# f32 routing tables, first expert's transposes inside its first half, and v cast behind its loads, in a fused attention and expert kernel

## The chip, the cores and the metric

The kernel runs on one core of a Trainium2 chip. The metric is the time of one execution on the device, in microseconds. The core has five engines that run their own instruction queues side by side: TensorE (PE, with its weight loads PEld), VectorE (DVE), ScalarE (ACT), GpSimd (POOL) and SyncE (SP). POOL, SP and ACT also issue DMA transfers.

## The reference

Block-causal attention over 8 batches, 8 heads, 576 positions and 64 channels, followed by a hard mixture of experts:

```python
scores = (1 / sqrt(64)) * q @ k.T                       # per batch and head
scores = where(pos[:, None] // 64 >= pos[None, :] // 64, scores, -1e9)
attn = exp(scores - max); attn = attn / sum(attn)
x = (attn @ v).transpose(0, 2, 1, 3).reshape(4608, 512) # 8 heads x 64 side by side
for e in range(8):                                      # each row has one expert
    rows = domain_id == e
    out[rows] = relu(x[rows] @ w1[e]) @ w2[e]           # 512 -> 1024 -> 512
```

The inputs and the output are f32; the kernel computes its matrix products on f16 operands.

## The kernel before, in words

The program is written in a fixed order: every engine executes its own instructions in the order in which the Python code emits them, and only semaphores hold it back.

**Attention** (lines 455 to 529) runs over 32 pairs of heads, four pairs to a batch, in 33 steps. In a step, PE computes the scores of pair p in three groups (`emit_G`, L348 and L374), ACT takes the exponential of each (`emit_exp`, L353), PE transposes q and k of pair p+2 (`emit_T`, L336), DVE copies those transposes out of PSUM (L340), and PE multiplies the weights of pair p-1 with v (`emit_pv`, L399 and L404, called by `emit_P` and `emit_Q`). DVE then divides by the row sums, which come from columns of ones in v (`emit_norm`, L427 and L428), and the rows x are stored to a DRAM buffer `x_rows` by SP (`store_x`, `store_w`).

v comes as f32 into one of three staging tiles `vst`, batch b into `vst[b % 3]`. Batch 0 is loaded by SP, all others by POOL, in nine transfers each (`load_v`, L79 and L83); POOL also issues the loads of q and k (`load_qk`, L70). `cast_v` (L115) makes f16 tiles `vS` of it in three instructions, on ACT for batch 0 and on POOL for the others. For the diagonal blocks of 64, `emit_VE` (L437) copies parts of v into a second tile `VE` with two DVE instructions a batch, which at present read `vS`. `loads(p)` at the end of step p sets the order on POOL: at step max(0, 4b-10) the q and k of batch b, five of its v transfers, the cast of batch b-1, and the remaining four transfers. At step 20 come the cast of the last batch and the weights of the first expert, one piece in each step up to 27.

**Routing.** In the first steps DVE counts for each row its place among the rows of its expert (`routing`). From step 2 on, `inverse` builds the table of row numbers per expert slot in slices between the steps: one-hot matrices `Hq`, `Hh` and `L` by comparisons and products on DVE (L204, L207, L211, L217), multiplied by PE (L229) and summed by DVE (L233, L235), then closed with L247 to L255. The operands `iota_h`, `lo_h` and `ub` and the matrices are f16.

**The last pair** (step 32) has its normalisation split by PSUM bank: `emit_norm(prev, 0, 1)` after `emit_P`, with a store, and `emit_norm(st, 1, 2)` after the last matmuls in `emit_Q`, with two stores. Then 36 dummy matmuls (`warm`, L533) keep PE running until the first rows are gathered.

**Experts.** For each of eight experts POOL gathers five blocks of 128 rows (L547), PE transposes them (`transpose_block`, L557) and ACT copies the result into `xT` (L560). `mm1` multiplies with w1 for eight column groups fc, with ACT applying ReLU into `hT` (L579, L585), and `mm2` with w2, block by block, while the next expert's blocks are transposed (L596); DVE copies the result out (L602) and POOL scatters it (L603). The first expert is done in two halves of 320 rows: blocks 0 to 2 are transposed and `mm1` runs on the first half, then blocks 3 and 4 and the second half. A loop at the end serves experts with more than 640 rows; its code is there, and on these inputs it does not run.

Of the kernel before, what the change touches and what calls it, by code (L numbers as in the profile page):

```python
# [9 lines left out]
F32 = mybir.dt.float32  # L10
F16 = mybir.dt.float16
# [7 lines left out]
def kernel(  # L19
# [82 lines left out]
    up = const.tile([128, 128], F16, name="up")  # L102
    make_upper_triangular(nc, up[:], 1.0, diag=False)
    load_qk(0, 1, HP)
    p_f = const.tile([128, 1], F32, name="p_f")
    nc.gpsimd.iota(out=p_f[:], pattern=[[0, 1]], base=4, channel_multiplier=NJ,
                   allow_small_or_imprecise_dtypes=True)
# [5 lines left out]
    def cast_v(fn, b):  # L113
        for pr, cs in ((128, slice(0, 2)), (128, slice(2, 4)), (64, slice(4, 5))):
            fn(  # L115
                out=vS[b % 3][0:pr, cs, :, 2:130],
                in_=vst[b % 3][0:pr, cs].rearrange(
                    "p c (g i) d -> p c g (i d)", i=2))
# [37 lines left out]


    ones_sq = const.tile([128, 128], F16, name="ones_sq")
    lo_h = const.tile([128, NJ], F16, name="lo_h")
    u_f = const.tile([128, NJ], F32, name="u_f")  # L160
    base_f = const.tile([128, 1], F32, name="base_f")
    n_i = const.tile([1, 1], I32, name="n_i")
# [25 lines left out]


    def inverse(sb, pp, tag, ncols, base, tok):  # L190
        ub = sb.tile([128, NJ], F16, name="ub", tag="ub")
        nc.vector.tensor_scalar(
            out=ub[:], in0=u_f[:], scalar1=base, scalar2=None, op0=ALU.subtract)
        inv = sb.tile([128, 2, ncols], F32, name="inv", tag="inv")
        fi = inv[:].rearrange("p a c -> p (a c)")
        sh = [128, NQ, ncols]
        ts = {}

        def hot(qt):
            js = slice(NQ * qt, NQ * qt + NQ)  # L200
            Hq = sb.tile([128, NQ, ncols], F16, name="Hq", tag="Hq", bufs=2)
            Hh = sb.tile([128, NQ, 2, ncols], F16, name="Hh", tag="Hh", bufs=2)
            L = sb.tile([128, NQ, 128], F16, name="L", tag="L", bufs=2)
            nc.vector.tensor_tensor(  # L204
                out=Hq[:], in0=iota_h[:, 0:ncols].unsqueeze(1).to_broadcast(sh),
                in1=ub[:, js].unsqueeze(2).to_broadcast(sh), op=ALU.is_equal)
            nc.vector.tensor_scalar(  # L207
                out=Hh[:, :, 0], in0=Hq[:], scalar1=p_f[:, 0:1], scalar2=None,
                op0=ALU.mult)
            yield  # L210
            nc.vector.tensor_tensor(  # L211
                out=Hh[:, :, 1], in0=Hq[:],
                in1=iota_h[:, js].unsqueeze(2).to_broadcast(sh), op=ALU.mult)
            yield
            for j in range(0, NQ, 3):
                sl = [128, 3, 128]
                nc.vector.tensor_tensor(  # L217
                    out=L[:, j : j + 3], in0=iota_h[:].unsqueeze(1).to_broadcast(sl),
                    in1=lo_h[:, js][:, j : j + 3].unsqueeze(2).to_broadcast(sl),
                    op=ALU.is_equal)  # L220
                yield
            ts[qt] = (L, Hh)

        def add(qt):
            L, Hh = ts[qt]
            ps = pp.tile([128, 512], F32, name=tag, tag=tag, bufs=2)
            pv = ps[:, 0 : 2 * ncols]
            for j in range(NQ):
                nc.tensor.matmul(  # L229
                    out=pv, lhsT=L[:, j], rhs=Hh[:, j].rearrange("p a c -> p (a c)"),  # L230
                    start=(j == 0), stop=(j == NQ - 1))
            if qt == 0:
                nc.vector.tensor_copy(out=fi, in_=pv)  # L233
            else:
                nc.vector.tensor_tensor(out=fi, in0=fi, in1=pv, op=ALU.add)  # L235

        for qt in range(4):
            first = True
            for _ in hot(qt):
                yield  # L240
                if first and qt:
                    add(qt - 1)
                first = False
        yield
        add(3)
        yield
        nc.vector.tensor_tensor(  # L247
            out=inv[:, 0], in0=inv[:, 0], in1=inv[:, 1], op=ALU.add)
        nc.vector.tensor_scalar(
            out=inv[:, 1], in0=inv[:, 0], scalar1=0.0, scalar2=1.0e6,  # L250
            op0=ALU.is_equal, op1=ALU.mult)
        nc.vector.scalar_tensor_tensor(
            out=tok[:, 0], in0=inv[:, 0], scalar=-4.0, in1=inv[:, 1],
            op0=ALU.add, op1=ALU.add)
        nc.vector.tensor_scalar(  # L255
            out=tok[:, 1], in0=tok[:, 0], scalar1=float(N - 1), scalar2=None,
            op0=ALU.min)
        yield
# [20 lines left out]
    def routing():  # L279
# [9 lines left out]
        for i, w in enumerate((ones_sq, up)):  # L289
# [24 lines left out]
        lo_i = asb.tile([128, NJ], I32, name="lo_i")  # L314
        nc.vector.tensor_scalar(out=lo_i[:], in0=ri[:], scalar1=127, scalar2=None,
                                op0=ALU.bitwise_and)
        nc.vector.tensor_copy(out=lo_h[:], in_=lo_i[:])
        nc.vector.tensor_scalar(out=cnt[:], in0=inc[:, :, NJ - 1], scalar1=-1.0,
                                scalar2=None, op0=ALU.add)
        nc.vector.memset(base_f[:], 0.0)  # L320
# [93 lines left out]
    def emit_Q(st):  # L414
        emit_pv(st, 3, 4)
        emit_pv(st, 4, 0)
        if st["p"] < npair - 1:
            emit_norm(st, 0, 2)
        else:
            emit_norm(st, 1, 2)  # L420

    def emit_norm(st, b0, b1):
        hp = st["p"] % HP
# [10 lines left out]
    def emit_VE(b):  # L434
        for i in range(2):
            cs = slice(2 + 64 * i, 66 + 64 * i)
            nc.vector.tensor_copy(  # L437
                out=VE[b % 2][64 * i : 64 * i + 64, :, :, cs],
                in_=vS[b % 3][0:64, :, :, cs])


    def store_w(b, w0, w1, c0, c1, eng):
# [20 lines left out]

    def loads(p):
        fn = nc.gpsimd.tensor_copy
        for b in range(2, B):
            if p == max(0, 4 * b - 10):
                load_qk(b)
                load_v(nc.gpsimd, b, range(0, 5))
                cast_v(fn, b - 1)  # L470
                load_v(nc.gpsimd, b, range(5, H + 1))
        if p == 4 * B - 12:
            cast_v(fn, B - 1)
            for e in range(4):
                wts.append(load_expert(e))
        if 4 * B - 12 <= p < 4 * B - 4:
            wts[0][p - 4 * B + 12]()
# [3 lines left out]
    for p in range(npair + 1):  # L481
# [13 lines left out]
            emit_G(1, st)  # L495
        if prev is not None:
            emit_P(prev)
            if prev["p"] == npair - 1:
                emit_norm(prev, 0, 1)
                store_w(B - 1, 0, 3, DM - 128, DM, nc.sync)  # L500
        if p < npair:
            emit_G(2, st)
        if prev is not None:
# [66 lines left out]
    def new_hT():  # L570
        return msb.tile([128, 8, CAP], F16, name="hT", tag="hT", bufs=2)

    def mm1(xT, hT, w1h, halves=(0, 1)):
        hw = CAP // 2
        for fc in range(8):
            ph = mps.tile([128, 2, 512], F32, name="ph", tag="ph", bufs=2)
            for dc in range(4):
                for i in halves:
# [56 lines left out]
    for e in range(E):  # L635
# [4 lines left out]
                f()  # L640
        hT = new_hT()
        if e == 0:
            for i, blks in enumerate(((0, 1, 2), (3, 4))):
                for blk in blks:
                    transpose_block(xgs[0], xT, blk)
                    if blk < 2:
                        warm(mps.tile([128, 512], F32, name="po", tag="po", bufs=2), 5)
                mm1(xT, hT, w1s[0], (i,))
        else:
            mm1(xT, hT, w1s[e])  # L650
        nxt = None
# [59 lines left out]
```

## Time and profile before

| | us |
|---|---|
| median of 4 runs | 322.93 |
| lowest, highest | 320.32, 325.6 |
| the profiled execution's own time | 318.33 |
| its span, first to last instruction | 316.6 |

| engine | busy us | share of the span | instructions |
|---|---|---|---|
| PE | 272.7 | 86% | 3668 |
| PEld | 177.1 | 56% | 3668 |
| DVE | 145.2 | 46% | 260 |
| ACT | 168.6 | 53% | 248 |
| POOL | 206.1 | 65% | 274 |

The shares are means over two stages: attention with the table until about 141 us, and the experts from about 150 us. The page also cuts the span into 40 slices; the view by stretches, used below, gives for a stretch the busy time of each engine with its number of instructions, the clock that was granted to PE, the mean busy share of the DMA engines and GB/s. In the view in order of time a row has its start, its duration, the engine, the line, the operation with its operands, how many instructions are joined in it, and in brackets the idle time of the engine just before it and what ended that. Matmuls are pipelined, so that a PE that is busy need not be at its peak.

### The profile page before, as it was taken

To read this page: it belongs to the slowest core of one execution; us is meant where nothing else is said; L and a number is where in the kernel's file an instruction comes from. 1 tells how busy PE (TensorE), PEld (TensorE's weight loads), DVE (VectorE), ACT (ScalarE), POOL (GpSimd) and SP (SyncE) were. 2 spreads that over 40 slices of the span, in tenths; PEclk is the share of its full clock that TensorE was granted. 3 is DMA by queue.
4 is the path that set the end of the run, shared out by engine and by line. 5 is a ranking of instruction groups with operands and counts; after the bars stand their busy time and mean duration, and the time that the engine had idled before them with its cause. 6 is when DMAs were issued, how large, how long until landed. Compare 5 with 4: busy or idle time off the path is not lost. (4 is left out here: it accounts for less than half of the span.)

```text
span 316.6 us, 8633 instructions
## 1 busy us (share of the span) xinstructions
PE 272.7 (86%) x3668; PEld 177.1 (56%) x3668; DVE 145.2 (46%) x260; ACT 168.6 (53%) x248; POOL 206.1 (65%) x274
## 2 busy tenths in 40 slices
PE   2598787959798999869989999999999999999920
PEld 1366565637575767644555656656565665756510
DVE  2878889999987888740003222030302203030210
ACT  5658575738777989840573444526344452635200
POOL 8659989899795800005888557878688686762230
PEclk9999798788989999998999999999999999999995
DMA  7999999997998593221788999898979989651120
GB/s 159 201 222 200 186 269 189 262 203 151 251 185 242 126 209 92 79 70 53 146 192 192 210 249 230 172 231 199 250 180 180 266 180 213 191 192 58 49 106 0
DMA packets 36488, 55.68 MB, mean 176 GB/s; under 512 B 9854, under 2 KB 22654, under 8 KB 36448
## 3 DMA queue, kind: packets, MB, share of 16 engines
q0 software_dynamic: 26128, 49.17, 72.5%
q1 hardware_dynamic: 10176, 5.90, 6.7%
q8 instruction: 30, 0.49, 0.6%
q14 instruction: 10, 0.08, 0.1%
q10 hardware_dynamic: 144, 0.03, 0.1%
HBM read 67.15 MB, written 15.20 MB: 260 GB/s over the span
## 5 line engine op out<-in xcount | busy, mean ns | idle before, releaser
L353 ACT ACTIVATE A<-ps 128x1024 f16<-128x1024 f32 (+1 forms) x96 | 83.1, 884 | 37.2 <-PE ps L348 25.7
L602 DVE COPY osb<-po 128x512 f32<-128x512 f32 x40 | 27.7, 692 | 132.6 <-PE po L596 104.3
L547 POOL DMA_INDIRECT xg<-x_rows,tok x40 | 40.6, 1015 | 47.6 <-issue 47.3
L585 ACT ACTIVATE hT<-ph 128x640 f16<-128x640 f32 (+1 forms) x72 | 46.4, 644 | 38.3 <-PE ph L579 37.4
L603 POOL DMA_INDIRECT out_dram<-osb,tok x40 | 40.7, 1017 | 34.7 <-DVE osb L602 17.6
L596 PE MATMUL po<-w2h,hT 128*128 128x512 f16 x240 | 56.7, 379 | 0.0
L579 PE MATMUL ph<-xT,w1h 128*128 128x320 f16 x384 | 54.2, 299 | 1.7 <-ACT xT L560 1.7
L79 POOL DMA_DIRECT2D vst<-in_v_dram x56 | 42.8, 791 | 11.4 <-DMA kh<-in_k_dram 5.8
L560 ACT COPY xT<-pt 128x512 f16<-128x512 f16 x40 | 23.3, 585 | 50.0 <-PE pt L557 37.2
L579 PEld LDWEIGHTS <-w1h 128*128 128x128 f16 x384 | 37.5, 98 | 18.1 <-issue 3.1
L340 DVE COPY QK<-PT 128x576 f16<-128x576 f16 x64 | 45.4, 749 | 3.3 <-PE PT L336 3.0
L596 PEld LDWEIGHTS <-hT 128*128 128x128 f16 x320 | 29.9, 98 | 29.3
L348 PE MATMUL ps<-QK 64*128 64x512 f16 (+3 forms) x256 | 36.8, 326 | 2.8 <-ACT A L353 1.1
L404 PE MATMUL po<-vS,A 128*128 128x65 f16 x640 | 36.5, 200 | 1.1 <-issue 1.1
L399 PE MATMUL po<-VE,ATE 128*128 128x130 f16 x160 | 32.7, 231 | 4.1 <-DVE x L428 4.0
L404 PEld LDWEIGHTS <-A 128*128 128x128 f16 x640 | 31.9, 102 | 4.6 <-issue 4.5
L428 DVE TENSOR_TENSOR x<-po,rc 128x768 f16<-128x768 f32 (+1 forms) x33 | 30.8, 933 | 1.1
L336 PE MATMUL PT<-identh,kh 64*64 64x64 f16 x576 | 17.2, 205 | 8.9 <-DVE inv L235 4.3
L336 PE MATMUL PT<-identh,qh 64*64 64x64 f16 x576 | 17.0, 205 | 5.1 <-DVE QK L340 3.7
L399 PEld LDWEIGHTS <-ATE 128*128 128x128 f16 x160 | 15.9, 99 | 9.5 <-issue 7.4
L336 PEld LDWEIGHTS <-kh 64*64 64x64 f16 x576 | 15.2, 120 | 10.3 <-issue 8.3
L336 PEld LDWEIGHTS <-qh 64*64 64x64 f16 x576 | 13.7, 118 | 12.8 <-issue 10.9
(89 smaller groups left out, 284.3 us busy)
## 6 DMA issues: line engine op xcount, KB each, us to landing
vst<-in_v_dram POOLq DMA_DIRECT2D x63, 128.0 KB, 7.0
w1h<-in_moe_w_dram POOLq DMA_DIRECT2D x24, 256.0 KB, 6.2
w2h<-in_moe_w_dram POOLq DMA_DIRECT2D x24, 256.0 KB, 8.4
vst<-in_moe_w_dram POOLq DMA_DIRECT2D x16, 256.0 KB, 8.7
qh<-in_q_dram POOLq DMA_DIRECT2D x14, 288.0 KB, 5.9
kh<-in_k_dram POOLq DMA_DIRECT2D x14, 288.0 KB, 8.3
x_rows<-x SPq DMA_DIRECT2D x7, 512.0 KB, 8.1
vst<-in_v_dram SPq DMA_DIRECT2D x4, 256.0 KB, 5.7
```

Of the source, the lines that this page charges most:

```text
L79: eng.dma_start(out=vst[b % 3][:, 0:4, n], in_=v[b, n, 0:512, :].rearrange("(c p) d -> p c d", p=128))
L336: nc.tensor.transpose(out=PT[h, j], in_=src[h, hp, 64 * j : 64 * j + 64], identity=identh[h, h])
L340: nc.vector.tensor_copy(out=QK[:, s].rearrange("p (n j) -> p n j", j=9), in_=PT[:].rearrange("p j n -> p n j"))
L348: nc.tensor.matmul(out=o[:, i], lhsT=QK[h, 1, 128 * c : 128 * c + 128], rhs=QK[h, 0, 64 + 128 * c : S], start=True, stop=True)
L353: nc.scalar.activation(out=o, in_=i, func=AF.Exp, scale=0.125)
L399: nc.tensor.matmul(out=o[:, 1:131], lhsT=st["AE"][:, 128 * m : 128 * m + 128], rhs=VE[b % 2][:, m, hp, 1:131], start=True, stop=(m == 0))
L404: nc.tensor.matmul(out=o[:, 1 + 65 * i : 66 + 65 * i], lhsT=at_block(st, i, c, m), rhs=vS[b % 3][:, c, hp, 1 + 65 * i : 66 + 65 * i], star ...
L547: nc.gpsimd.indirect_dma_start(out=g[:, blk, :], out_offset=None, in_=xd, in_offset=bass.IndirectOffsetOnAxis(ap=tok[:, 1, blk : blk + 1], ...
L579: nc.tensor.matmul(out=ph[:, i, 0:hw], lhsT=w1_cols(w1h, dc, fc), rhs=xT[:, dc, hw * i : hw * i + hw], start=(dc == 0), stop=(dc == 3))
L585: nc.scalar.activation(out=hT[:, fc].rearrange("p (i n) -> p i n", i=2)[:, i0:i1], in_=ph[:, i0:i1, 0:hw], func=AF.Relu)
L596: nc.tensor.matmul(out=po[:], lhsT=hT[:, fc, 128 * blk : 128 * blk + 128], rhs=w2h[:, fc, :], start=(fc == 0), stop=(fc == 7))
L603: nc.gpsimd.indirect_dma_start(out=dst[blk], out_offset=bass.IndirectOffsetOnAxis(ap=tok[:, 0, blk : blk + 1], axis=0), in_=osb[:], in_off ...
```

## The change

Five things are edited. The tables `Hq`, `ub` and `lo` and the iota that they are compared with become f32 (a second iota on POOL); `Hh` and `L`, which PE reads, stay f16. `emit_VE` reads the f32 staging tile in batches 0 to 5, and `vS` only in the last two. `loads` issues all nine v transfers of a batch together and casts batch b at step max(1, 4b-4). The first normalisation of the last pair and its store move behind the last matmuls, into `emit_Q`. And the transposes of the first expert's blocks 3 and 4 are issued inside the first half's `mm1`, ahead of column groups 4 and 6.

```diff
+    iota_f = const.tile([128, 128], F32, name="iota_f")
+    nc.gpsimd.iota(out=iota_f[:], pattern=[[1, 128]], base=0, channel_multiplier=0,
+                   allow_small_or_imprecise_dtypes=True)
...
-    lo_h = const.tile([128, NJ], F16, name="lo_h")
+    lo_f = const.tile([128, NJ], F32, name="lo_f")
...
-        ub = sb.tile([128, NJ], F16, name="ub", tag="ub")
+        ub = sb.tile([128, NJ], F32, name="ub", tag="ub")
...
-            Hq = sb.tile([128, NQ, ncols], F16, name="Hq", tag="Hq", bufs=2)
+            Hq = sb.tile([128, NQ, ncols], F32, name="Hq", tag="Hq", bufs=2)
...
-                out=Hq[:], in0=iota_h[:, 0:ncols].unsqueeze(1).to_broadcast(sh),
+                out=Hq[:], in0=iota_f[:, 0:ncols].unsqueeze(1).to_broadcast(sh),
...
-                in1=iota_h[:, js].unsqueeze(2).to_broadcast(sh), op=ALU.mult)
+                in1=iota_f[:, js].unsqueeze(2).to_broadcast(sh), op=ALU.mult)
...
-                    out=L[:, j : j + 3], in0=iota_h[:].unsqueeze(1).to_broadcast(sl),
-                    in1=lo_h[:, js][:, j : j + 3].unsqueeze(2).to_broadcast(sl),
+                    out=L[:, j : j + 3], in0=iota_f[:].unsqueeze(1).to_broadcast(sl),
+                    in1=lo_f[:, js][:, j : j + 3].unsqueeze(2).to_broadcast(sl),
...
         if st["p"] < npair - 1:
             emit_norm(st, 0, 2)
-        else:
-            emit_norm(st, 1, 2)
+            return
+        emit_norm(st, 0, 1)
+        store_w(B - 1, 0, 3, DM - 128, DM, nc.sync)
+        emit_norm(st, 1, 2)
...
                 out=VE[b % 2][64 * i : 64 * i + 64, :, :, cs],
-                in_=vS[b % 3][0:64, :, :, cs])
+                in_=vst[b % 3][0:64].rearrange(
+                    "p c (g i) d -> p c g i d", i=2)[:, :, :, i]
+                if b < B - 2 else vS[b % 3][0:64, :, :, cs])
...
-        for b in range(2, B):
-            if p == max(0, 4 * b - 10):
+        for b in range(1, B):
+            if b > 1 and p == max(0, 4 * b - 10):
                 load_qk(b)
-                load_v(nc.gpsimd, b, range(0, 5))
-                cast_v(fn, b - 1)
-                load_v(nc.gpsimd, b, range(5, H + 1))
+                load_v(nc.gpsimd, b, range(H + 1))
+            if p == max(1, 4 * b - 4):
+                cast_v(fn, b)
         if p == 4 * B - 12:
-            cast_v(fn, B - 1)
             for e in range(4):
...
-            if prev["p"] == npair - 1:
-                emit_norm(prev, 0, 1)
-                store_w(B - 1, 0, 3, DM - 128, DM, nc.sync)
...
-    def mm1(xT, hT, w1h, halves=(0, 1)):
+    def mm1(xT, hT, w1h, halves=(0, 1), between={}):
         hw = CAP // 2
         for fc in range(8):
+            if fc in between:
+                between[fc]()
...
-            for i, blks in enumerate(((0, 1, 2), (3, 4))):
-                for blk in blks:
-                    transpose_block(xgs[0], xT, blk)
-                    if blk < 2:
-                        warm(mps.tile([128, 512], F32, name="po", tag="po", bufs=2), 5)
-                mm1(xT, hT, w1s[0], (i,))
+            for blk in range(3):
+                transpose_block(xgs[0], xT, blk)
+                if blk < 2:
+                    warm(mps.tile([128, 512], F32, name="po", tag="po", bufs=2), 5)
+            mm1(xT, hT, w1s[0], (0,), {
+                4: lambda: transpose_block(xgs[0], xT, 3),
+                6: lambda: transpose_block(xgs[0], xT, 4)})
+            mm1(xT, hT, w1s[0], (1,))
```

The instructions on POOL, as built, change only so: in every batch the three casts stand behind all nine v transfers rather than behind five, and the last batch's casts stand behind the four w1 pieces of the first expert.

## The prediction

> **What bounds the kernel now.** I read the page first. Its chain of what ended last is no help, since it holds only the final 1.1 us, so I took the table by stretches and then the instructions in order of time.
>
> ```profile
> 40.00:60.00 20.00, 16.54 (x375) 12.16 (x369) 19.01 (x32) 13.00 (x18) 18.55 (x26) 0.83 1.08 247
> 60.00:80.00 20.00, 15.99 (x387) 11.86 (x385) 19.17 (x32) 13.30 (x20) 18.50 (x26) 0.91 0.96 184
> 120.00:140.00 20.00, 16.63 (x393) 12.21 (x392) 14.06 (x25) 16.62 (x24) 0.00 (x0) 1.00 0.15 49
> 200.00:240.00 40.00, 40.00 (x273) 24.74 (x272) 6.92 (x10) 19.07 (x30) 31.02 (x39) 1.00 0.94 206
> ```
>
> After the span the columns are PE, PEld, DVE, ACT, POOL. From 40 to 80 us DVE is busy for 38.2 of 40 us: while the routing table is built beside attention, DVE sets the pace. At 120 to 140, with the table and the loads done, a pair takes 3.0 us (the reciprocals of L427 at 131.51, 134.50, 137.50), with ACT busiest; a pair with an L437 copy still costs about 0.5 us in each of two steps (112.31 to 115.78 to 119.32 us between multiplications). So DVE time added before 105 us lengthens attention nearly one for one. From 180 to 280 us PE is full, and what starts the first expert earlier ends the kernel earlier.
>
> Part of DVE's time is not work. Its rows, then POOL's:
>
> ```profile
> 41.29 0.52 DVE L211 TENSOR_TENSOR Hh<-Hq,iota_h 128x360 f16<-128x360 f16 x1
> 53.45 3.63 DVE L211 TENSOR_TENSOR Hh<-Hq,iota_h 128x360 f16<-128x360 f16 x1
> 66.66 2.56 DVE L437 COPY VE<-vS 64x1280 f16<-64x1280 f16 x2
> 80.69 2.03 DVE L247 TENSOR_TENSOR inv<-inv 128x40 f32<-128x40 f32 x1
> 126.18 0.97 DVE L437 COPY VE<-vS 64x1280 f16<-64x1280 f16 x2
> 31.82 1.09 DVE L437 COPY VE<-vS 64x1280 f16<-64x1280 f16 x2 [0.84 <-POOL vS L115]
> ```
>
> ```profile
> 54.02 2.67 POOL L115 CAST vS<-vst 128x1024 f16<-128x1024 f32 x3
> 67.51 3.47 POOL L115 CAST vS<-vst 128x1024 f16<-128x1024 f32 x3
> 80.00 2.66 POOL L115 CAST vS<-vst 128x1024 f16<-128x1024 f32 x3
> 33.53 0.75 POOL L79 DMA_DIRECT2D vst<-in_v_dram  x1 [0.17 <-issue]
> ```
>
> The same L211 takes 0.52 us, or 3.63 when POOL's three casts run beside it, and it ends just after they do; L437 and L247 stretch in the same way. Operations that read PSUM (L340, L427, L428) do not. I count the loss as 3.1 at 53 us; 1.6 for L437 at 66 and, just behind it, 0.6 for L211 and 0.4 for L217; 2.1 at 81 to 83 (L247 and L249 against some 0.2 and 0.3); 0.5 for L437 at 86, beside a load. That is **8.3 us**, and 0.84 us more where the L437 copy waits for the cast outright.
>
> **The change, part by part.**
>
> *VE copied from the f32 staging tile (batches 0 to 5).* Twelve L437 copies, median 488 ns each with f16 input. Instructions of 360 (L204, 526 ns) and 384 elements (L217, 549 ns) give about 1 ns an element over some 150 ns fixed; so the f16 copy moves 1280 elements in 338 ns, four an element time. No DVE copy from f32 in SBUF is in the trace. It is bounded by 0.49 us (nothing changes) and by one element per ns, 1280 + 150 = 1.43 us. I take the value nearest to the same copy: equal bytes per ns, 2 x 338 + 150 = 0.83 us, 0.34 more. 12 x 0.34 = **+4.0 us** (0 to +11.3). All lie before 102 us and count in full. The wait on the cast goes: **-0.84 us**. Next behind it would be the load of v for batch 1, issued by 22.3 and, at 7 us to landing, there by about 29, before 31 us.
>
> *f32 tables.* The L204, L211 and L217 instructions (20 in all) already run at one element per ns; L309, 288 elements with an f32 input, takes 457 ns, the same rate. So nothing for them. L207, four times 399 ns for 360 elements, is faster than that rate; at L211's 524 ns it costs 4 x 0.125 = **+0.5 us** (0 to +0.5). The one iota more on POOL (0.33 us, like L98) stands at 7.7 us before loads that wait for transfers anyway (0.94 us at 11.22): nothing.
> The Trainium skill, "VectorE: DVE Perf Modes", section "The perf-mode tier table", speaks against this edit: two-input operations run at twice the f32 rate on 16-bit data. By it each L217 would take half its element time, and f32 would cost 20 x some 0.2 = 4 us. The row says 549 ns for 384 elements with 16-bit data, so there is nothing to lose; the operand that is broadcast is the likely reason. I go by the row.
>
> *Casts after all nine loads of v.* The order on POOL changes only so: a batch's three casts (2.66 us) move behind four more loads, and the last batch's behind four w1 pieces. As built, a load waits for the landing of the load eight issues before. Now the cast fills that wait (only 0.17 us idle at 33.53); afterwards it does not. The last load ends at 34.96, and the first cast starts there rather than at 29.12, so the q and k loads behind it slip by 2.7 us, in every batch. They are used far later (batch 3 is loaded at 35 and transposed from about 60 us): nothing. vS of batch 1 is ready at 37.6, its last part that PE reads at 37.0; PE reads it between 36.5 and 37.1: 0 (0 to +1.0).
> What moves is where casts meet DVE. I walk both engines forward with the durations above, a POOL round of about 14 us: casts at about 35, 49, 63.5, 80 and 95 us. They then meet an L217 (0.5 us), the batch 2 copy (2.3) and a table block (1.2), and nothing afterwards: 4.1 us instead of 8.3. But two of these five land within half a microsecond of an edge, so I take half of the gain: **-2.1 us** (-8.3 if no cast meets anything; +7.2 if five casts each cost the 3.1 seen at 53 us).
> A second rule, the box on DVE and SWDGE in "SBUF — State Buffer", section "SBUF: two separate sides", says that an f32 copy within SBUF keeps POOL from writing the descriptors of its loads. At 47.87, beside L437, two loads still take 1.28 us as elsewhere. By the rule POOL would lose up to 12 x 0.34 = 4 us, all of it before its idle 35 us at 110; no end moves.
>
> *First expert's transposes.*
>
> ```profile
> 158.82 0.61 PE L557 MATMUL pt<-identh,xg 128*128 128x128 f16 x8
> 159.35 1.07 ACT L560 COPY xT<-pt 128x512 f16<-128x512 f16 x2
> 160.48 4.94 PE L579 MATMUL ph<-xT,w1h 128*128 128x320 f16 x32 [1.04 <-ACT xT L560]
> ```
>
> Set inside the first half, the eight transposes cost PE the same, and the copies (0.58 us) lie between ReLUs that leave ACT 0.12 us free in each 0.62 us; a copy holds one ReLU back, and the second ph buffer covers that. Blocks 3 and 4 were requested at 149.55 and 150.85; with 4.4 us to land they are there by 155.3, before the new places at about 156.5 and 158. The 1.04 us wait goes: **-1.0 us** (0 to -1.2). The second half is then bound by PE.
>
> *Last pair's normalisation.*
>
> ```profile
> 140.36 0.22 PE L399 MATMUL po<-VE,ATE 128*128 128x130 f16 x1 [0.88 <-DVE x L428]
> 140.91 0.20 DVE L427 RECIPROCAL rc<-po 128x6 f32<-128x6 f32 x1 [0.61 <-PE po L399]
> 145.50 1.10 POOL L547 DMA_INDIRECT xg<-x_rows,tok  x1 [35.73 <-issue]
> ```
>
> PE's last nine matmuls no longer wait; the first normalisation now waits for them instead, since the second has no wait left. It starts about 0.55 us later, its store on SP at 140.9 instead of 140.33; behind that store queues only the one of 141.72. The second normalisation still ends near 141.6, and the gathers need all stores. The dummy matmuls of L533 start and end 0.6 us earlier, which lets the first transposes start when their rows land (their load is ready at 149.95, they run at 150.38): **-0.3 us** (+0.6 to -0.6).
>
> **Sum:** 4.0 - 0.84 + 0.5 - 2.1 - 1.0 - 0.3 = +0.3 us on the profiled execution's 318.3 us. That one is 4.6 us under the 322.93 median of the runs; on the median the forecast is **323.2 us**.
>
> **Rivals.** (1) *The f32 copy has no fast form*: 1.43 us each, 11.3 instead of 4.0, so +7.6: **330.5 us**. It makes the kernel slower by 1% from 1.07 us a copy (2.9 us more over twelve). For it: no f32 copy of this kind in the trace; against it: the f16 one runs four times the plain rate from strided rows. (2) *The casts land on the copies*: L437 comes once per batch, so do the casts, and both may lock together as at 66 us; five meetings at 3.1 give 15.5 instead of 6.2, so +9.6: **332.5 us**, half of it at half the meetings. It decides once casts meet DVE for more than the present 8.3 us. (3) *The casts miss everything*: -8.3 instead of -2.1, so -5.9: **317.0 us**. For it: the casts at 42.11 and 93.85 miss today; against: DVE has SBUF work in nearly every step of the table. (4) *The casts hardly move*, if landings speed up and POOL does not wait: collisions stay, +2.4: **325.3 us**.
>
> **How the numbers follow.** Forecast 0.45, alone 320 to 326.5; (1) 0.13; (2) 0.15, as a whole or in part; (3) 0.13; (4) 0.14. Runs of this kernel tell about 1% from no change, 3.2 us. Faster: all of (3) and a twelfth of the forecast's weight, 0.17. Slower: (1), most of (2), and 0.10 from the tails of forecast and (4), 0.36. Same: 0.47. The range takes in (1) and half of (2), and stops just above (3): 317.5 to 331.
>
> **What would show it.** L437's copies from vst near 0.83 us right, near 1.4 means (1); L207 near 0.52 and L217 still 0.55; no wait on ACT before the first expert's second half; and long L211, L217, L437 or L247 only beside POOL's casts, about 4 to 6 us in all. The forecast is wrong above all if the casts fall elsewhere than I walked them.

## The result, and the profile after

| | before | after |
|---|---|---|
| median, us | 321.06 (15 runs) | 322.68 (10 runs) |
| lowest, highest, us | 314.69, 325.6 | 321.86, 325.15 |
| ratio after / before | | 1.0207 [1.0151, 1.0263] |
| the profiled execution, us | 318.33 | 325.09 |
| last normalisation ends, us | 141.70 | 150.31 |
| from there to the end of the span, us | 174.9 | 173.1 |

The ratio leaves out executions more than 1.5% above the fastest of their kernel, so that it sets all ten of after against the three quickest of the fifteen of before and says 2.1% where the medians differ by 0.5%; of profiled executions below that were such ones, only times are read (the tail alone, the direct loads without the tail, the two edits on v alone), and rows too of one, the second profile of before. The quotient of the means over all executions is 1.005 here, 1.7 us; it stands below behind each ratio as "all". The change makes the kernel slower, by 2% in the ratio and by 0.5% over all executions; the forecast was +0.3 us. The two profiled executions lie apart by more than that, 6.8 us, since the one of before is among its quicker runs and the one of after among its slower.

The stage that changed is attention: its last normalisation ends 8.6 us later, and the experts give 1.85 us back. The view by stretches of the changed kernel has the columns span, PE, PEld, DVE, ACT, POOL, granted clock of PE, DMA share and GB/s:

```profile
40.00:60.00 20.00, 15.50 (x349) 11.43 (x343) 17.93 (x32) 11.79 (x16) 16.41 (x22) 0.84 0.89 183
60.00:80.00 20.00, 16.70 (x355) 11.98 (x350) 16.14 (x28) 12.15 (x17) 15.56 (x22) 0.79 1.04 220
120.00:140.00 20.00, 17.56 (x429) 12.83 (x426) 15.12 (x25) 15.15 (x21) 0.50 (x1) 0.91 0.47 96
200.00:240.00 40.00, 40.00 (x272) 24.77 (x271) 7.61 (x11) 18.15 (x28) 30.28 (x37) 1.00 0.96 213
```

From 40 to 80 us DVE is busy for 34.1 us where it was 38.2, and yet PE gets fewer matmuls done (704 instead of 762). The clock at 60 to 80 is 0.79 instead of 0.91, and at 120 to 140, where nothing was edited, 0.91 instead of 1.00. DVE's busy time up to the last normalisation is 115.8 us against 115.9 before. **The sum on DVE came out as worked; attention did not follow it.**

In order of time, DVE's rows behind that sum:

```profile
32.99 1.66 DVE L442 CAST VE<-vst 64x1280 f16<-64x1280 f32 x2
34.69 3.42 DVE L220 TENSOR_TENSOR L<-iota_f,lo_f 128x384 f16<-128x384 f32 x2
44.58 0.53 DVE L207 TENSOR_TENSOR Hq<-iota_f,ub 128x360 f32<-128x360 f32 x1
45.14 0.59 DVE L210 TENSOR_SCALAR Hh<-Hq,p_f 128x360 f16<-128x360 f32 x1
52.92 2.26 DVE L442 CAST VE<-vst 64x1280 f16<-64x1280 f32 x2
```

and POOL's casts:

```profile
35.66 2.92 POOL L118 CAST vS<-vst 128x1024 f16<-128x1024 f32 x3
51.31 3.18 POOL L118 CAST vS<-vst 128x1024 f16<-128x1024 f32 x3
66.06 2.58 POOL L118 CAST vS<-vst 128x1024 f16<-128x1024 f32 x3
```

(Lines have moved: L442 is the old L437, L220 the old L217, L207 and L210 the old L204 and L207, L118 the old L115, L232 and L238 the old L229 and L235, L339 and L343 the old L336 and L340, L402 and L407 the old L399 and L404, L584 the old L579.) The copy from f32 takes 0.83 us, without a wait. The L220 pair at 34.69 takes 3.42 instead of 1.09 us beside a cast; it stands ahead of the copy out of PSUM that PE waits for. PE's rows in order of time show what comes of it, and two waits of another kind:

```profile
38.83 0.69 PE L339 MATMUL PT<-identh,qh 64*64 64x64 f16 x18 [3.70 <-DVE QK L343]
53.47 0.31 PE L339 MATMUL PT<-identh,kh 64*64 64x64 f16 x9 [1.23 <-issue]
57.55 0.48 PE L232 MATMUL PT<-Hh,L 128*128 128x80 f16 x9 [1.82 <-DVE QK L343]
74.56 0.47 PE L339 MATMUL PT<-identh,kh 64*64 64x64 f16 x18 [2.51 <-DVE inv L238]
111.49 0.47 PE L339 MATMUL PT<-identh,kh 64*64 64x64 f16 x18 [1.85 <-DVE QK L343]
129.47 0.22 PE L402 MATMUL po<-VE,ATE 128*128 128x130 f16 x1 [1.33 <-issue]
165.95 6.22 PE L584 MATMUL ph<-xT,w1h 128*128 128x320 f16 x40
```

The bracket is PE's idle time before the row. Behind the 3.70 us the same 18 transposes take 0.69 instead of 0.47 us: PE's clock is down to 0.5 (half clock) from 37.9 to 44.7 us. The waits at 53.47 and 129.47 end with "issue": every operand was there. The one at 111.49 is put down to DVE's copy, but that had ended at 110.85; it stands at a matmul number at which PE waits for instructions (last section). The last row has no wait any more: the 1.04 us for ACT is gone.

The same rows in the profile of before, for comparison:

```profile
34.68 0.47 PE L336 MATMUL PT<-identh,qh 64*64 64x64 f16 x18 [1.65 <-DVE QK L340]
69.55 0.64 PE L336 MATMUL PT<-identh,kh 64*64 64x64 f16 x17 [3.34 <-DVE inv L235]
101.78 0.25 PE L404 MATMUL po<-vS,A 128*128 128x65 f16 x3 [1.11 <-issue]
```

Between the reciprocals of pairs 0 and 8, 8 and 20, and 20 and 28, before took 36.0, 47.7 and 25.5 us, after 39.0, 45.5 and 31.5. The first stretch has the 3.70 us pause, the last one the two instruction waits of 1.85 and 1.33 us. In that last stretch the same 650 matmuls are busy for 27.22 instead of 24.36 us, by the clock, and PE is idle for 4.29 instead of 1.10: 2.86 + 3.19 make up the 6.05 us.

### The profile page after: what moved, and what is told of

The parts are those of the page before. It is cut to its first block, busy times and chain, and to the rows that moved or that the text cites. A ratio compares the mean times of both kernels' runs of the same rounds, so it can differ in the third digit from the quotient of the medians.

```text
span 323.4 us, 8656 instructions
## 1 busy us (share of the span) xinstructions
PE 273.2 (84%) x3668; PEld 178.0 (55%) x3668; DVE 144.9 (45%) x260; ACT 168.9 (52%) x248; POOL 207.4 (64%) x275
## 5 line engine op out<-in xcount | busy, mean ns | idle before, releaser
L608 POOL DMA_INDIRECT out_dram<-osb,tok x40 | 40.7, 1017 | 31.0 <-DVE osb L607 14.4
L584 PE MATMUL ph<-xT,w1h 128*128 128x320 f16 x384 | 54.2, 299 | 0.7 <-ACT xT L563 0.7
L343 DVE COPY QK<-PT 128x576 f16<-128x576 f16 x64 | 45.5, 749 | 5.4 <-PE PT L339 5.1
L584 PEld LDWEIGHTS <-w1h 128*128 128x128 f16 x384 | 37.5, 98 | 16.7 <-issue 1.8
L407 PE MATMUL po<-vS,A 128*128 128x65 f16 x640 | 36.9, 201 | 0.3 <-issue 0.3
L402 PE MATMUL po<-VE,ATE 128*128 128x130 f16 x160 | 33.1, 233 | 4.5 <-DVE x L433 3.2
L407 PEld LDWEIGHTS <-A 128*128 128x128 f16 x640 | 32.3, 103 | 2.6 <-issue 2.6
L339 PE MATMUL PT<-identh,kh 64*64 64x64 f16 x576 | 17.7, 206 | 11.0 <-DVE inv L238 3.5
L339 PE MATMUL PT<-identh,qh 64*64 64x64 f16 x576 | 17.4, 208 | 8.1 <-DVE QK L343 7.2
L339 PEld LDWEIGHTS <-qh 64*64 64x64 f16 x576 | 14.2, 121 | 16.1 <-issue 14.1
L339 PEld LDWEIGHTS <-kh 64*64 64x64 f16 x576 | 15.5, 121 | 12.5 <-issue 9.8
L402 PEld LDWEIGHTS <-ATE 128*128 128x128 f16 x160 | 16.0, 100 | 9.8 <-issue 7.5
```

Source lines behind the costliest of these rows:

```text
L339: nc.tensor.transpose(out=PT[h, j], in_=src[h, hp, 64 * j : 64 * j + 64], identity=identh[h, h])
L343: nc.vector.tensor_copy(out=QK[:, s].rearrange("p (n j) -> p n j", j=9), in_=PT[:].rearrange("p j n -> p n j"))
L402: nc.tensor.matmul(out=o[:, 1:131], lhsT=st["AE"][:, 128 * m : 128 * m + 128], rhs=VE[b % 2][:, m, hp, 1:131], start=True, stop=(m == 0))
L407: nc.tensor.matmul(out=o[:, 1 + 65 * i : 66 + 65 * i], lhsT=at_block(st, i, c, m), rhs=vS[b % 3][:, c, hp, 1 + 65 * i : 66 + 65 * i], star ...
L584: nc.tensor.matmul(out=ph[:, i, 0:hw], lhsT=w1_cols(w1h, dc, fc), rhs=xT[:, dc, hw * i : hw * i + hw], start=(dc == 0), stop=(dc == 3))
L608: nc.gpsimd.indirect_dma_start(out=dst[blk], out_offset=bass.IndirectOffsetOnAxis(ap=tok[:, 0, blk : blk + 1], axis=0), in_=osb[:], in_off ...
```

## The experiments

Two theories stood against each other. **The theory of the sum**: attention follows DVE's busy time, as the prediction had it. **The theory of the late loads**: with the casts behind them the loads of v end later (the last is issued at 110.5 instead of 99.8 us), and while transfers are in flight PE waits longer for its instructions, from 105 us on. Ratios are to executions of before on the same chip, and times are compared only between runs on one chip: on the two chips on which before takes 332 to 334 us, the time behind the last normalisation alone is 10 to 15 us longer.

### The tail alone

```diff
+        emit_norm(st, 0, 1)
+        store_w(B - 1, 0, 3, DM - 128, DM, nc.sync)
+        emit_norm(st, 1, 2)
...
-                emit_norm(prev, 0, 1)
-                store_w(B - 1, 0, 3, DM - 128, DM, nc.sync)
...
-                mm1(xT, hT, w1s[0], (i,))
+            mm1(xT, hT, w1s[0], (0,), {
+                4: lambda: transpose_block(xgs[0], xT, 3),
+                6: lambda: transpose_block(xgs[0], xT, 4)})
+            mm1(xT, hT, w1s[0], (1,))
```

> Only the two edits behind attention: the first expert's transposes inside its first half, and the last pair's normalisation behind the matmuls. If the loss of the whole change lies in attention alone, this one is faster by what the tail of the changed kernel shows: 11.20 to 9.90 us from the first half's start to the next transposes (-1.3), and 12.35 to 11.80 us from the last normalisation's end to that start (-0.55), so -1.9 us or a ratio of 0.994. If the rows gathered are late again after the earlier end of the dummy matmuls, only -1.3 us, 0.996. Attention itself as before: the last normalisation ends within 1.5 us of 141.7.

332.27 us against 332.50, ratio 1.0004 [0.9931, 1.0077] (all: 1.000). The 1.3 to 1.9 us expected of it are within the interval, and so is nothing. That attention would end within 1.5 us of 141.7 was missed: in the one profile, the longest of its twelve executions, it ended at 148.9, with nothing edited ahead of the last pair. What the tail gives is read better behind the last normalisation: 174.9 us to the end of the span in before and 173.1 in after, and, on the chip of the second profile of before, 161.8 us to PE's last matmul in before and 160.0 with direct loads and this tail.

### The f32 copies alone

```diff
-                in_=vS[b % 3][0:64, :, :, cs])
+                in_=vst[b % 3][0:64].rearrange(
+                    "p c (g i) d -> p c g i d", i=2)[:, :, :, i]
+                if b < B - 2 else vS[b % 3][0:64, :, :, cs])
```

> Only the copies into VE from the f32 staging tile, casts in their old places on POOL. Theory of the sum (DVE's time decides): twelve copies of 0.82 instead of 0.49 us, +4.0, less the 0.84 us wait at 31 us: +3.2 us, ratio 1.010, with the casts meeting DVE for 6 to 10 us in all. Theory of the late loads (the loss after 105 us comes from loads that still run there): the loads end as before near 110 us, so PE loses no more than the 1.9 us that it loses before at every 128th matmul, and everything lost is lost by 105 us.

337.38 us, ratio 1.0232 [1.0092, 1.0373], which is 3 to 12 us (all: 1.015, 4.9 us). The sum's +3.2 lies at the lower end, so the copies cost what the sum says or more; this run does not speak against it. In this profile PE pauses for 4.74 us at 57.91, behind a copy that a cast stretched (+1.2 us) and two table operations (+0.7 and +0.8).

### Everything but the casts' new place

```diff
-                load_v(nc.gpsimd, b, range(H + 1))
-            if p == max(1, 4 * b - 4):
-                cast_v(fn, b)
+                load_v(nc.gpsimd, b, range(0, 5))
+                cast_v(fn, b - 1)
+                load_v(nc.gpsimd, b, range(5, H + 1))
```

(This diff is against after.)

> The whole change except the place of the casts on POOL: f32 tables, f32 copies, the two edits behind attention. Theory of the sum: +4.0 for copies, +0.75 for the four L207 forms at 0.59 us, -0.84 for the wait, -1.9 behind attention: +2.0 us, ratio 1.006, give or take the meetings of casts and DVE (3 us). Theory of the late loads: POOL's last load of q, k, v is back at about 100 us, so the stretch from 105 to 135 us takes 3 to 5 us less than in the changed kernel, and the kernel is 4 us faster than the changed one (ratio to before about 1.00 to 1.01).

334.94 us against 332.50, with too few runs for a ratio (all: 1.008): some +2.4 us, which is near the sum's +2.0. Pairs 20 to 28 take 26.5 us, without a half clock.

### The changed kernel on another chip

No edit against after.

> The whole change again, unaltered, for a second profile of it beside the same runs of the kernel before. If the loss after 105 us belongs to the change (its loads end 8 to 10 us later than before), PE again waits for more than 1 us at two or more of the 128th matmuls between 105 and 135 us, and the ratio lies at 1.015 to 1.025. If those waits come and go from one execution to the next, the second profile has them at other places or not at all, and the ratio lies within 1% of no change. DVE's excess from meeting casts, 3.7 us in the first profile, stays at 3 to 6 us under both.

336.94 us against 333.75, ratio 1.0176 [1.0077, 1.0275] (all: 1.012). It is slower here too. Pairs 20 to 28 take 29.2 us: one instruction wait of 1.83 us and one stretch at half clock.

### More loads late

```diff
+        if p == 4 * B - 5:
+            junk = asb.tile([128, 5, Fdim], F16, name="junk")
+            for i in range(12):
+                nc.gpsimd.dma_start(out=junk[:, i % 5],
+                    in_=moe_w1[4 + i // 4][128 * (i % 4) : 128 * (i % 4) + 128, :])
```

(Against before; nothing reads `junk`, so the output stays and only loads are added.)

> The kernel before with twelve further transfers of 0.5 MB each from DRAM into a tile that nobody reads, issued by POOL right after the first expert's weights; they add nothing that any engine waits for before the gathers. If PE's waits at the 128th matmuls come from transfers in flight, then two or more of the four marks between 110 and 135 us now show waits above 0.7 us, and attention ends 2 to 6 us later than in the kernel before. If they have another cause, attention ends within 1 us of the kernel before.

332.58 us in one run, against 333.75. Pairs 20 to 28 take 29.1 us instead of 25.5, with waits of 0.62 and 1.33 us for instructions at 121.67 and 127.86 and one stretch at half clock. That spoke for the late loads; the late casts alone, below, do not.

### Before, from another chip

No edit.

> The kernel before, unchanged, for a profile of it from another chip. Both theories: the 36.0 us between the reciprocals of pairs 0 and 8 and the 25.5 us between those of pairs 20 and 28 (first profile of before) come back within 1.5 us, and PE's waits at every 128th matmul after 105 us sum to under 2 us. If pairs 20 to 28 take 28 us or more here, the late stretch of the changed kernel is no mark of its late loads.

324.38 us, against a median of 320.93 on this chip and 2.5% above the quickest there. Pairs 20 to 28 take 26.6 us, as expected; but pairs 0 to 8 take 42.0 us, not 36.0, and the last normalisation ends at 147.3 instead of 141.7: the same program, with 117.2 us of DVE time against 115.9. In order of time, on DVE

```profile
28.89 2.87 DVE L211 TENSOR_TENSOR Hh<-Hq,iota_h 128x360 f16<-128x360 f16 x1
41.87 2.44 DVE L204 TENSOR_TENSOR Hq<-iota_h,ub 128x360 f16<-128x360 f16 x1
54.05 3.06 DVE L437 COPY VE<-vS 64x1280 f16<-64x1280 f16 x2
```

and on PE

```profile
32.48 0.47 PE L336 MATMUL PT<-identh,qh 64*64 64x64 f16 x18 [2.68 <-DVE QK L340]
44.95 0.69 PE L336 MATMUL PT<-identh,kh 64*64 64x64 f16 x18 [3.22 <-DVE inv L233]
59.29 0.76 PE L229 MATMUL PT<-Hh,L 128*128 128x80 f16 x9 [3.43 <-DVE QK L340]
```

The casts start within 1.6 us of the first profile's for the first four batches, but they meet other instructions, and those stand ahead of something that PE waits for. With 1.3 us more of DVE attention is 5.6 us longer, in one and the same program: where a cast hits counts, and not only how many microseconds of DVE it costs. That the theory of the sum falls does not rest on this one execution, but on the runs that follow.

### The late casts alone

```diff
-                load_v(nc.gpsimd, b, range(0, 5))
-                cast_v(fn, b - 1)
-                load_v(nc.gpsimd, b, range(5, H + 1))
+                load_v(nc.gpsimd, b, range(H + 1))
+            if p == max(1, 4 * b - 4):
+                cast_v(fn, b)
```

> Only the casts move behind all nine loads of their batch; the copies into VE still read the f16 tile. Theory of the sum (DVE's time decides): the casts' meetings with DVE fall from 8.4 us to about 4, nothing is added, so about 4.5 us faster, ratio 0.986. Theory of the late loads: the same gain before 100 us, but pairs 20 to 28 take 29 us or more instead of 25.5, with PE waiting at its 128th matmuls, so some 1 us faster or nothing, ratio 0.997 to 1.003.

324.87 us, ratio 1.0202 [1.0115, 1.0289] (all: 1.012, 3.8 us): neither theory had it slower. DVE's busy time to the last normalisation falls to 110.7 us, as the sum wanted, and pairs 20 to 28 take 25.9 us with the last v load at 108.2, as late as in the changed kernel within 2.3 us. **So in this profile the late loads do not lengthen the late stretch, and the theory that they always do falls.** What both overlooked is the first copy into VE, which now waits for the late cast, first on DVE and then on PE:

```profile
38.06 0.99 DVE L437 COPY VE<-vS 64x1280 f16<-64x1280 f16 x2 [6.52 <-POOL vS L115]
```

```profile
40.83 0.69 PE L336 MATMUL PT<-identh,qh 64*64 64x64 f16 x18 [7.23 <-DVE QK L340]
```

and a stretch of 10.2 us at half clock from 36.9 us. This wait is what the f32 copies avoid in the full change. A sum that counted it like the 0.84 us of before, 5.7 us more, would have said +1.2 us instead of -4.5; so this run refutes the sum as it was made up, but hardly the rate of one for one.

### Both edits on v, without tables and tail

The diffs of the copies and of the casts together.

> The late casts and the f32 copies together, without the f32 tables and without the edits at the tail. Theory of the sum: +4.0 for the copies, -0.84 for the wait, -4.5 for the meetings, so 1.3 us faster, ratio 0.996. Theory of the late loads, with the copies' cost as the f32 copies alone showed it (ratio 1.023): 5 to 7 us slower, ratio 1.015 to 1.02, pairs 0 to 8 in 38 us or more and pairs 20 to 28 in 28 us or more.

324.32 us, ratio 1.0144 [1.0067, 1.0222] (all: 1.012). The sum's 0.996 is outside. So the loss of the whole change is there with the two edits on v alone; the f32 tables and the tail are not needed for it.

### Without casts: the loads write f16

For batches 1 to 7 the transfers convert on their way and write into the tile that PE reads, without staging and without POOL's casts; batch 0 stays as it was. There are four `vS` tiles instead of three.

```diff
-                    out=vst[b % 3][:, 0:4, n],
+                    out=vS[b % 4][:, 0:4, g, 2 + 64 * i : 66 + 64 * i],
...
-                cast_v(fn, b - 1)
```

> The kernel before without any cast on POOL: the transfers of v for batches 1 to 7 write f16 straight into vS (four of these tiles instead of three, ten transfers a batch instead of nine); all else as before. This removes what casts cost DVE: the 8.3 us counted and the 0.84 us wait. Theory of the sum: -7 to -9 us, ratio 0.972 to 0.978. If the casts' meetings with DVE cost the kernel little because other waits take their place: within 3 us, ratio above 0.99. If PE's waits at every 128th matmul depend on how busy the transfers are, they appear at other places, since POOL no longer pauses between loads.

328.95 us, ratio 0.9928 [0.9854, 1.0002] (all: 0.989). The sum's 0.972 to 0.978 is outside: some 8 us of DVE taken away gave less than half as much. With the edits at the tail as well:

> The kernel before with v brought as f16 straight into four vS tiles (no casts on POOL), with the two edits behind attention. Theory of the sum: -8 us for the casts' meetings with DVE and -1.9 behind attention, ratio 0.970. With the waits at the 128th matmuls as in the first try of the direct loads (8.2 us instead of 2 to 3): about -4 us, ratio 0.985 to 0.990.

329.13 us, ratio 0.9939 [0.9843, 1.0034] (all: 0.988), on the chip on which the changed kernel had 1.0176. The same kernel again, on another chip and with more executions:

> The kernel whose loads write f16 straight into the tile that PE reads (no casts, no f32 tile, four buffers) with the edits at the tail, once more and with more rounds. Theory of the sum: without casts DVE loses nothing to them (8.4 us) and the tail gives 1.5 us, so 8 us or more faster, ratio 0.975. Theory of the late loads: pairs 20 to 28 take 29 us or more and give 3 to 5 us of that back: ratio 0.985 to 0.995, as its first run had (0.994).

316.46 us against 320.93, ratio **0.9904 [0.9852, 0.9955]** (all: 0.986): faster than both kernels. DVE's busy time to the last normalisation is 108.3 us, some 8 us less than in before, and attention ends at 140.8 us. The sum's 0.975 is outside. Of what the profiled executions differ, the tail has some 2 us (174.9 and 175.4 us behind the last normalisation in the two profiles of before, 173.1 here); the rest, 0.9 us against the first and 6.5 against the second, lies in attention. There the gain is in the first pairs: 0 to 8 take 32.3 us, where before took 36.0 and 42.0; pairs 20 to 28 take 29.9, with an instruction wait of 2.13 us, and give some back. The stretches of pairs 0 to 8 and 20 to 28, first of this kernel,

```profile
22.92:55.17 32.25, 26.44 (x668) 19.57 (x666) 29.14 (x54) 23.10 (x32) 24.57 (x37) 1.00 1.33 151
101.08:130.97 29.89, 27.03 (x650) 19.71 (x649) 22.15 (x37) 22.96 (x33) 6.99 (x12) 0.89 0.85 134
```

then of the changed one:

```profile
24.47:63.43 38.96, 29.64 (x668) 21.89 (x666) 33.83 (x55) 23.48 (x33) 30.75 (x41) 0.85 0.89 173
108.96:140.47 31.51, 27.22 (x650) 19.79 (x649) 22.03 (x37) 23.26 (x33) 10.79 (x16) 0.89 0.58 123
```

The same 668 matmuls take 26.44 us of PE at clock 1.00 and 29.64 at 0.85. The 6.7 us between the first rows are 3.2 of slower clock and 3.5 of PE standing idle.

### Three tiles instead of four

```diff
-    vS = [asb.tile([128, 5, HP, 132], F16, name=f"vS{i}") for i in range(4)]
+    vS = [asb.tile([128, 5, HP, 132], F16, name=f"vS{i}") for i in range(3)]
```

With three tiles the load of batch b stands in program order ahead of the last pairs' multiplications of batch b-3, so those pairs wait for it and multiply with the v of the later batch: part of the computation is changed, and the time holds that wait.

> The same with three vS tiles, so that the loads of batch b wait until batch b-3 has been multiplied, and are spread over the whole of attention instead of running as fast as the transfers allow. If PE's waits at every 128th matmul come from transfers that run without a pause, they fall below 4 us here, and the ratio is 0.970 to 0.980. If the loads now come too late, PE or DVE waits for the transfers of q, k or v in attention, and the ratio is above 0.99.

360.21 us, ratio 1.0859 [1.0777, 1.0941]. PE's row for the first of these waits:

```profile
47.86 0.50 PE L407 MATMUL po<-vS,A 128*128 128x65 f16 x2 [19.74 <-DMA vS<-in_v_dram]
```

PE's clock is at half for 20.5 us from 31.3 on. The run says nothing on how loads are best spread; it only shows that the fourth tile is needed.

### What the profiles say together

Ten profiles, with times from the rows in order of time (from the first pair's reciprocal to the second's), busy times from the view by stretches, and the time at half clock from the granted clock in the trace:

| kernel | pairs 0-8, us | of it at half clock | pairs 20-28, us | of it at half clock | DVE busy to the last normalisation | that ends at |
|---|---|---|---|---|---|---|
| before | 36.0 | 9.3 | 25.5 | 0 | 115.9 | 141.7 |
| before, other chip | 42.0 | 17.1 | 26.6 | 0 | 117.2 | 147.3 |
| before, more loads | 36.1 | 7.8 | 29.1 | 3.4 | 113.1 | 143.9 |
| f32 copies alone | 39.5 | 10.2 | 27.0 | 0 | 120.6 | 150.2 |
| all but the casts | 38.2 | 10.0 | 26.5 | 0 | 116.5 | 147.8 |
| late casts alone | 41.8 | 14.4 | 25.9 | 0 | 110.7 | 146.9 |
| after | 39.0 | 11.9 | 31.5 | 6.8 | 115.8 | 150.3 |
| after, other chip | 39.6 | 11.4 | 29.2 | 3.4 | 116.0 | 148.2 |
| direct, tail | 32.3 | 0 | 29.1 | 3.4 | 108.2 | 140.8 |
| direct, tail, other chip | 32.3 | 0 | 29.9 | 6.8 | 108.3 | 140.8 |

Over the ten, the first stretch takes 32.0 us + 0.61 for each us at half clock (a straight line fits with R² 0.94; 0.93 without the second profile of before, 0.83 without the two kernels with direct loads). The line does not part the half clock from the pauses that bring it: between the first rows of the two views above, 11.9 us at half clock cost 3.2 us of slower matmuls, and the rest is pauses. DVE's time orders the kernels badly: the late casts alone have 110.7 us and end at 146.9, before has 115.9 and ends at 141.7.

## Why the prediction was right or wrong, point by point

**The f32 copies, +4.0 us.** 0.805 at least and 0.821 in the median, against 0.83 foretold: twelve times 0.33 over the f16 copy is 4.0 us of DVE. Rival (1), one element per ns, falls. What 4 us of DVE are worth is another matter, below.

**The wait on the cast, -0.84 us.** Gone, as foretold. With the late casts it would have become 6.52 us on DVE; the two edits on v need each other, which the prediction did not say.

**The f32 tables, +0.5.** L210 (the old L207) takes 587 against 400 ns, four times 0.19 = 0.75 us: the row taken as the upper end, L211 with its 524, was none. The others are unchanged at 526 and about 550 ns. So the row was right about the two-input operations, and the 4 us that the prediction estimated from the Trainium skill's tier table ("VectorE: DVE Perf Modes", section "The perf-mode tier table") are not there. Why these operations gain nothing from 16 bits no run shows; that it is the broadcast operand stays a guess.

**The casts' meetings with DVE, 8.3 to 4.1, half taken: -2.1.** The walk put the casts at about 35, 49, 63.5, 80 and 95 us; they start at 35.66, 51.31, 66.06, 80.44 and 95.08. The meetings sum to 3.7 us (L220 at 34.69 +2.3, L442 at 52.92 +0.6, two L220 +0.7), against 8.4 by the same count in before. The walk was good and the full -4.7 came; taking half was the mis-sized term. Rivals (2), (3) and (4) fall with it: the copies lose 0.6 us, where that rival had 15.5; something is met; the casts do move.

**Lateness of the casts on PE, 0.** No row of PE in attention waits for `vS`. Right. That POOL loses time to the copies into VE does show, against what the prediction read off one row: the load at 72.53, inside the copies at 72.50, takes 1.09 us, where a load beside no copy takes 0.75 and at most 0.84; in the second profile of after one takes 1.36. The load at 34.22, near the end of the copies at 32.99, takes 0.75. The trace of before has such a load too, 0.98 us at 31.64. From 20 us on it is some 1 us in all in after, less than the 4 us that the prediction allowed for.

**The transposes, -1.0, and the last pair, -0.3.** From the first half's start to the next transposes 9.90 instead of 11.20 us, -1.3; from the last normalisation to the first half 11.80 instead of 12.35, -0.55. Both right in kind and somewhat larger.

**The sum.** With every term at its measured size it is 4.0 - 0.84 + 0.75 - 4.7 - 1.3 - 0.55 = -2.6 us. The profiled executions differ by +6.8 us, and the means over all executions by +1.7 us on the first chip and +4.0 on the second. **The step that failed is "So DVE time added before 105 us lengthens attention nearly one for one"**, in the part on what bounds the kernel, and with it the subtraction of removed DVE time at the same rate. Added DVE time cost what the sum says or more (the copies alone, all but the casts); it is the removed time that gave less than half (some 8 us of it without casts) or nothing (both edits on v, 0.996 foretold, 1.0144 measured). The rate was read off stretches in which DVE is busy for 95%. But those rows also had the granted clock at 0.83 and 0.91, and the prediction quoted them and made nothing of them. (Nor is ACT the busiest from 120 to 140: PE has 16.63 us there, ACT 16.62.) What the runs showed instead: in the first pairs, attention goes by PE's pauses together with the half clock behind them. DVE time that stands ahead of something PE is waiting for becomes a pause: the cast's first meeting, +2.3 us on L220, makes one of 3.70 us, with 6.8 us at half clock behind it. What DVE time elsewhere costs was not measured by itself. How the 4.7 us taken off the meetings divide between the two kinds is not measured; the first meeting at least moved to a worse place.

**The 0 for the loads that go out earlier and end later.** The prediction had no term for PE's instruction waits. They took 1.85 and 1.33 us of the changed kernel's late stretch, which with the clock behind them is 6 us longer; in its second profile 1.83. Yet the late casts alone, with the same late loads, show 0.76 there. So these waits are real and are part of the profiled difference, but that the change causes them is not shown.

**The number.** The forecast of 323.2 us is within 0.5 us of the median of 322.68, and that is chance: the median of before in the new runs was 1.9 us lower than in the first four, and the change cost 1.6 us between the medians where 0.3 was forecast. The range of 317.5 to 331 held the median because it was made for casts that fall unluckily, which is akin to what happened, though not by the prices of the rivals.

**Open.** How large the loss is: 0.5% over all executions on the first chip, 1.2% on the second, 2.1% and 1.8% in the ratios. Two profiles of before and two of after are too few to divide it between the early pauses and the instruction waits. The copies alone (1.0232) and both edits on v (1.0144) place it in the edits on v, with intervals that overlap; that it goes by the pauses is read from the rows, and no run took the pauses alone away.

## What to carry to other kernels

Where PE runs in short bursts between other engines, look for the PE pauses that an edit makes or removes and for the half clock behind them; the busy sum of the engine with the highest share is a poor measure of what removed work gives, even at 95%. Rather than move conversions to where they hopefully hit less, take them out: moving the casts alone lost 2.0% (all: 1.2%), and loads that write f16 gave 0.7%, with an interval that just touches nothing (all: 1.1%), and 1.0% (all: 1.4%) together with the tail. And profile the unchanged kernel twice before explaining a difference of a few us: here the same program's attention ended at 141.7 and 147.3 us.

## What the runs showed of the hardware

**The clock falls when PE is busy for less than some 60% of 3.4 us.** In the ten profiles, between 25 and 135 us, PE paused 22 times for 0.8 to 1.3 us, and 3 of these were followed by half clock; of 24 pauses of 1.3 to 2 us 15 were, of 20 longer ones 18. All 36 stretches at half clock begin inside such a pause or at most 2.5 us behind it; they last 3.41 us or a multiple, and begin on a grid of that step. Counted by the steps of this grid the rule is sharper: of the 271 steps at full clock from 25 to 140 us PE was busy for 61% or less in 42, and 36 of these were followed by half clock (all 30 below 58%); of the 229 busier ones none was. In after, PE is busy for 0.67 of the 3.41 us from 34.46, around the pause of 3.70 us, and the clock is at half from 37.87. So a pause counts by how much of it falls into one step, some 1.4 us being enough, and shorter ones in one step add up: in before the half clock from 86.56 us follows a longest pause of 0.92 us, with PE busy for 58% of the step. The Trainium skill ("TensorE: Matmul & The Clock Gate", section "What's actually happening") has the clock fall after an idle window of about 3.4 us. The length of the windows agrees with the trace; the idle time that suffices is shorter here.

**PE waits for instructions at fixed places.** Of PE's waits of 0.5 us or more that end with "issue" before 145 us, all 30 in the ten profiles stand at matmul number 96 + 128k, to within one record. PE issues a weight load with each matmul, so that is every 256 instructions. The page of the changed kernel lists the transfers:

```profile
q8 instruction: 30, 0.49, 0.6%
```

30 packets and 0.49 MB, 16 KB each; 3668 matmuls with as many weight loads make 28.7 times 256. The Trainium skill ("Advanced Engine Details and Errata", section "ISA Cache") gives a line of 16 KB or 256 instructions, which agrees; it has no figure for the wait. Here it was 0.5 to 2.5 us where it showed at all. What makes it long is open: the two longest, 2.48 and 2.13 us, are in the kernels with direct loads, whose DMA share is highest, but the one run that added loads showed at most 1.33.
